# Transform work of the next batch in the drained accumulator banks: two first-stage groups or one second stage at a group's second step

## The chip, the cores and the metric

One core of one Trainium2 chip runs the kernel. The time is device microseconds of that core for one execution. The engines named below are TensorE (PE in the profile; its weight loads are PEld), VectorE (DVE), ScalarE (ACT), GpSimd (POOL) and SyncE (SP), which here issues nearly all DMAs. An engine works through its own instructions in program order and waits for others by semaphores. TensorE writes its results to PSUM, eight banks of 128 partitions by 512 fp32 numbers; ScalarE and VectorE read them there.

## The reference

```python
batch, seq, dim = (8, 3008, 256)          # d_ff = 2048, everything fp32
X = np.fft.fft(x, axis=1)
X = np.fft.fft(X, axis=2)
a = X.real.astype(np.float32)             # (8, 3008, 256) -> (24064, 256)
h = a @ w_in                              # w_in (256, 2048)
g = h * (1.0 / (1.0 + np.exp(-1.702 * h)))
out = (g @ w_out).astype(np.float32)      # w_out (2048, 256)
```

A Fourier transform over the sequence and the model dimension, of which the real part is kept, then a two-layer block with a quick GELU.

## The kernel before, in words

**Tiling.** The sequence of 3008 is 47 x 64. The transform over it is made in two stages. The *first stage* (`mix1`, L251) combines the factor 47; the *second stage* (`stage2`, L381) combines the factor 64. The transform over the model dimension is folded into `w_in` beforehand (`wcs`), so that the second stage's result `pq` is multiplied by `wcs` directly. A batch of 3008 tokens is cut into 3 blocks, a block into 2 halves, a half (a *group*) into 8 *steps* p = 0 to 7, each with two of the 16 slices of the 2048 hidden columns. That makes 48 steps a batch and 384 in all (`steps`, indexed by t; t0 = 48 b is the first step of batch b). The first 8 steps have a form of their own; t >= 8 run the loop described here. A step's tile has 256 columns, 226 in the second half of block 0.

**A step t.** PE: `begin(t, 1)` finishes the hidden values of t in a bank x (`b0` or `b1`, by t's parity), the three large products of step t-3 (`product`, with LAG = 3) go to the banks `o0` and `o1`, and `begin(t + 1)` starts the next step's hidden values. ACT: `forward` (L642), in a group's second step after it also the three copies of `swap` (L836 to L838), then `doubled` (L639), `activate_back` (L649) and `middle(t + 2)` (L627, two instructions), which writes a bias into the bank that `begin(t + 2)` will add to. DVE: `backward` (L646), the sums for the products (L664, L665; `deeper` L688, L690, L692), at a group's end the combination of its results (`combine` L799, L800; `combine_small` L828; `combine_last` L810, L846) and the transposition of the output (L779). POOL: sums (L657, L658) and the folding of the next batch's input (`fold1`).

**Small products.** The product with `w_out` is made by a fast scheme of two levels. For each pair of steps PE makes 28 products of 64 x 128 (`small_products`, L702, matmuls at L726), seven kinds k of four each, 56 instructions on the chip. They gather over a group in the tile `low`, which is three banks, and for k = 1 in half of `o1`. They go in two parts: k = 1, 2, 4, 7 three steps after the pair's second step, k = 5, 6, 3 one step later. `combine_small` reads `low` when a group has ended; from then on until the next group's first small products the three banks hold nothing that is needed. `start` of a matmul (`first_in`) clears what a bank holds.

**The next batch.** While batch b is multiplied, batch b+1 is prepared by functions that the table `extra` (filled by `at`, from `PLANS`) calls at the end of certain steps: 16 folds on POOL, 4 first-stage groups `mix1` on PE, whose result of two banks two copies on ACT (`mixed`, L279) bring back to `xt` (the first at once, the second in the next step), `spill` to DRAM, `fill` from DRAM into `t4`, `rotate`, and per block a second stage, whose two banks two transpositions on DVE (L399) bring to `pq`. `nyquist_out` and `nyquist` carry one row of it through DRAM and spread it over all partitions. `paced` is a tiny DMA that holds SP's queue until a step's activation is made. `spill`, `fill`, `load_x`, the Nyquist row and the stores are DMAs in SP's queue, in the order in which they are called.

**Banks for that.** PSUM's eight banks are `o0`, `o1`, `b0`, `b1`, `b2` and the three of `low`. A step in which `mix1` or `stage2` is called is *special*, the step after it is *after*. In a special step the two banks for it are `b2` and the x bank of step t. As that bank is not free, `middle(t + 2)` is put off to the next step, and in that step the small products are dealt out differently:

```python
if after and t + 1 < n:
    middle(t + 1)
...
cut = 0 if opening and not after else 3 if after else 2
...
if t + 2 < n and not special:
    middle(t + 2)
...
spare[:] = [f"b{t % 2}"] * special + ["b2"]
```

`opening` is the first step in which a new group's products run, that is (t - 3) % 8 == 0. Before, in batches 1 to 6, `mix1` is called at t0+7, 15, 23 and 31, and `stage2` at t0+8, 24 and 40.

Of the kernel before, what the change touches and what calls it, by code (L numbers as in the profile page):

```python
# [44 lines left out]
LAG = 3  # L45
# [76 lines left out]
def kernel(ctx: ExitStack, tc, x, w_in, w_out, tab1, tab2, out):  # L122
# [56 lines left out]
    def bank(name, tag=None):  # L179
        if tag is None:  # L180
            tag = spare.pop(0)
            spare.append(tag)
        if tag in ("o0", "o1"):
            return o_banks[int(tag[1])]
        return (rest if tag[0] == "o" else psp).tile([128, 512], F32, tag=tag, name=name)


# [88 lines left out]
    waiting = []  # L276

    def mixed(m, r, ps):
        nc.scalar.copy(free(xt[:], (4 * m + r) * D, [2 * D, 2], [1, D]), free(ps[:], 0, [D, 2], [1, D]))  # L279
# [122 lines left out]
    def nyquist(b, blk):  # L402

        nb = nbt[b, blk] = pqp.tile([128, 512], F32, tag="nb", name="nb")
        if (b, blk) != (0, 0):
            nc.sync.dma_start(out=nb[:], in_=view(Nd, (b * NBLK + blk) * 512, [0, 128], [1, 512]))
            return
        ps = bank("psn")
        halves(ps[:], ones[:], pqt[b, blk][:, 1, :], start=True, stop=True)
        nc.scalar.copy(nb[:], ps[:])  # L410


    def nyquist_out(b, blk):
        i = b * NBLK + blk
        nc.sync.dma_start(out=Nd[i:i + 1, :], in_=pqt[b, blk][0:1, 1, :])

# [140 lines left out]
    def width(t):  # L557

        return 226 if steps[t][1:3] == (0, 1) else 256
# [136 lines left out]
    def spot(pair_, k):  # L696
        return 256 + 128 * pair_ if k == 1 else 768 * pair_ + 128 * SPOT[k]

    def both(k, *dims):
        return free((o_banks[1] if k == 1 else pot["low"])[:], spot(0, k), [spot(1, k) - spot(0, k), 2], *dims)  # L700

    def small_products(t, ks):  # L702

        if t < 0 or not deep(t) or not steps[t][3] % 2:
            return
        p, w = steps[t][3] - 1, width(t) // 2
        for k in ks:
            for pr in range(2):
                for side in range(2):
                    op_ = 2 * pr + side  # L710
                    weights, q = ((wo, 2), (wo, 3), (wt, 2), (wt, 3))[op_]
                    y0, y1 = (weights[:, p + i, q, :] for i in range(2))
                    at = MADE + (p // 2 * 2 + pr) * 512 + side * 64
                    lhs = {1: y0[:, 0:64], 2: y1[:, 0:64], 3: y1[:, 64:128]}.get(k)
                    if lhs is None:
                        at += {5: 0, 6: 1, 7: 2, 4: 3}[k] * 128
                        lhs = big[:, at:at + 64]
                    raw_ = {1: (t - 1, 0), 2: (t, 0), 4: (t, 1)}.get(k)
                    if raw_:
                        rhs = right(raw_[0], op_, 256)[:, raw_[1] * w:raw_[1] * w + w]  # L720
                    else:
                        i0 = SUM + 512 * {7: 0, 5: 1, 6: 2, 3: 3}[k] + 128 * op_
                        rhs = big[:, i0:i0 + w]
                    first_in = p == 0 and (k, pr) in ((2, 0), (2, 1), (4, 1))
                    o = (o_banks[1] if k == 1 else pot["low"])[64 * side:64 * side + 64, spot(pr, k):spot(pr, k) + w]
                    nc.tensor.matmul(o, lhsT=lhs, rhs=rhs, start=first_in, stop=(p == NP - 2), skip_group_check=True)  # L726

    def small_weights(n):
# [227 lines left out]
    for h0 in (0, 512):  # L956
# [10 lines left out]
    halved(1)  # L967

    extra = {}
    PLANS = (((*range(9, 18), 22, 23, 24, 25, 26, 29, 30), (15, 17, 26, 31), 33),  # L970
             ([g + k for g in (0, 8, 16, 24) for k in range(-2, 2)], (7, 15, 23, 31), 33))

    def at(t, fn, *args):
        extra.setdefault(t, []).append((fn, args))
# [20 lines left out]
    for b in range(B):  # L995
        t0 = b * NBLK * NF
        if b + 2 < B:
            for k in range(3):
                at(t0 + 11 + k, paced, t0 + 11 + k)
                at(t0 + 11 + k, turn, b + 2, k)  # L1000
        if b + 1 < B:
            folds, groups, filled = PLANS[min(b, 1)]
            for c in range(NCH):
                for part in range(2):
                    at(t0 + folds[2 * c + part], fold1, b + 1, c, part, nc.gpsimd)
                if c % 2:
                    k = t0 + groups[c // 2]
                    at(k, mix1, b + 1, c // 2)
                    for half in range(2):
                        at(k + 1, spill, b + 1, half, c // 2)  # L1010
            for blk in range(NBLK):
                at(t0 + filled + blk, paced, t0 + filled + blk)
                at(t0 + filled + blk, fill, b + 1, 4 * blk, 4 * blk + 4)
            if b + 2 < B:
                for k in range(4):
                    at(t0 + 36 + 2 * k, paced, t0 + 36 + 2 * k)
                    at(t0 + 36 + 2 * k, load_x, b + 2, k)
                at(t0 + 34, paced, t0 + 34)
                at(t0 + 34, load_ends, b + 2)
                at(t0 + 41, fold_ends, b + 2, nc.gpsimd)  # L1020
            at(t0 + 39, rotate, b + 1)
        for blk in range(NBLK):
            nxt = (b, blk + 1) if blk + 1 < NBLK else (b + 1, 0)
            if nxt[0] < B:
                at(t0 + blk * NF + 8, stage2, *nxt)
                at(t0 + blk * NF + 9, nyquist_out, *nxt)
                at(t0 + blk * NF + 10, nyquist, *nxt)

    SCRIPT = (
        [(nyquist, 0, 0), (fold_w, 1, ("o0", "o1")), (prepare, out0), (rows, 0, ((sizes, out0, nc.vector), (clamp, out0))), (high, out0)],  # L1030
# [8 lines left out]
    for t in range(n + LAG):  # L1039
        if t < NP:  # L1040
            if t == NP - 3:
                spare[:] = [tag for tag in spare if tag[0] == "o"] + ["b2"]
            if t == NP - 1:
                middle(NP)
            hidden(t)
            if t == NP - 1:
                begin(NP)
                no_row(1024)
            for fn, *args in SCRIPT[t]:
                fn(*args)  # L1050
            if t == NP - 1:
                doubled(NP)
                middle(NP + 1)
        else:
            after, special = (any(fn in (mix1, stage2) for fn, _ in extra.get(k, ())) for k in (t - 1, t))
            if t < n:
                begin(t, 1)
            if t == NP:
                activate(t - 1)
            if after and t + 1 < n:  # L1060
                middle(t + 1)
            if t < n:
                forward(t)
            while waiting:
                m, ps = waiting.pop()
                mixed(m, 1, ps)
            opening = (t - LAG) % NP == 0 and t >= NP + LAG
            one, other = (t - LAG, (1, 2, 4, 7)), (t - LAG - 1, (5, 6, 3))
            if opening:
                small_products(*other)  # L1070
            cut = 0 if opening and not after else 3 if after else 2
            product(t - LAG, 0, cut)
            if after:
                small_products(one[0], one[1][:1])
                small_products(other[0], () if opening else other[1][:1])
            if t + 1 < n:
                begin(t + 1)
            if not opening:
                small_products(other[0], other[1][after:])
            product(t - LAG, cut, 6 if t - LAG == last else None)  # L1080
            small_products(one[0], one[1][after:])
            swap(t - LAG - 2)
            if t < n:
                backward(t)
            if t + 1 < n:
                doubled(t + 1)
            if t < n:
                activate_back(t)
                sums(t, nc.gpsimd)
            if t + 2 < n and not special:  # L1090
                middle(t + 2)
            combine_small(t - LAG - 1)
            if t - LAG == last:
                product(last, 6, None)
            sums(t - 1, nc.vector)
            deeper(t - 2, 0)
            deeper(t - 3, 1)
        if t == NP:
            psu.close()
            low = ctx.enter_context(tc.tile_pool(name="low", bufs=1, space=PS))  # L1100
            pot["low"] = low.tile([128, 3 * 512], F32, tag="low", name="low")
        if t >= LAG:
            combine(t - LAG)
            combine_last(t - LAG - 2)
            turn_last(t - LAG - 3, 0)
            turn_last(t - LAG - 4, 1)
        if t >= NP:
            spare[:] = [f"b{t % 2}"] * special + ["b2"]
        for fn, args in extra.get(t, ()):
            fn(*args)  # L1110

# [27 lines left out]
```

## Time and profile before

| | |
|---|---|
| runs | 1843.16, 1844.06, 1845.63 us; median 1844.06 us |
| profiled execution | 1846.94 us, span on the core 1845.2 us |
| granted PE clock | 0.999 |
| DVE busy | 1477.5 us (80% of the span) |
| ACT busy | 1137.2 us (62%) |
| POOL busy | 998.3 us (54%) |
| first-stage matmuls, L271, 47x256 | 434 instructions on the chip, mean 388 ns |
| second-stage matmuls, L392, 64x128 | 1536 instructions, mean 278 ns |
| first-stage copies on ACT, L279 | 56, mean 580 ns |
| second-stage transpositions on DVE, L399, 128x512 | 46, mean 696 ns |
| DMA | 105.95 MB, mean 57 GB/s |

The shares are of the span. A line of the order in time gives start, length, engine, line, operation, what it writes and reads, shape and count; in brackets the engine's idle time before it and who ended that. Neighbouring instructions of one kind are merged. One matmul of the program is two instructions on the chip, and two column halves run side by side, so lengths of matmuls overlap, and what a group costs is read from start to start.

### The profile page before, as it was taken

The page shows a single profiled execution, that of the slowest core. Times are in us where ns is not written, and L with a number is a line of the kernel's source. Part 1 is how long each engine was busy: PE and PEld are TensorE (multiplying, and loading weights), DVE is VectorE, ACT ScalarE, POOL GpSimd, SP SyncE. Part 2 cuts the span into 40 slices and gives each one's busy share as a digit, 9 for nine tenths or more (in the row PEclk, how much of TensorE's full clock was granted, in tenths as well). Part 3 has the DMA queues.
Part 4 walks back from the last instruction along what each step waited for, and adds up shares of the span by engine and source line. Part 5 has one row for each costly group of instructions (what it writes and reads, how often), then busy time and mean ns, then how long its engine had stood idle before and what let it go on. Part 6 is the DMA issues. An engine that isn't in the chain of part 4 may idle for free.

```text
span 1845.2 us, 55857 instructions
## 1 busy us (share of the span) xinstructions
PE 1827.1 (99%) x23652; PEld 1398.2 (76%) x23652; DVE 1477.5 (80%) x1934; ACT 1137.2 (62%) x2230; POOL 998.3 (54%) x1070
## 2 busy tenths in 40 slices
PE   8999999999999999999999999999999999999998
PEld 4677777777777777777777777777777777778776
DVE  6878888887888778877888778877888788878874
ACT  3666666666666666666566666666666666556663
POOL 3785556654656546564456644656446654444442
PEclk9999999999999999999999999999999999999999
DMA  8821341114211151211502115020241102100001
GB/s 263 202 70 26 86 69 28 55 32 100 49 45 43 33 114 30 60 33 42 116 14 72 30 52 97 20 74 26 71 76 27 31 26 58 29 19 13 23 19 24
DMA packets 151833, 105.95 MB, mean 57 GB/s; under 512 B 106229, under 2 KB 133111, under 8 KB 151024
## 3 DMA queue, kind: packets, MB, share of 16 engines
q1 hardware_dynamic: 148416, 99.35, 22.4%
q8 instruction: 186, 3.05, 0.7%
q10 hardware_dynamic: 3168, 3.03, 0.6%
q14 instruction: 63, 0.52, 0.1%
HBM read 65.07 MB, written 48.05 MB: 61 GB/s over the span
## 4 chain that ended last, share of the span: by engine, by line
PE 92%; POOL 2%; DVE 2%; DMA 2%; issue 2%; ACT 0%; SPq 0%; DVEq 0%; POOLq 0%; ACTq 0%
PE x L194 34%; PE o L194 25%; PE low L726 25%; PE o L726 4%; PE ps L271 2%; PE ps L392 1%; DMA big<-in_moe_w_in_dram 1%; DMA xt<-in_x_dram 1%; POOL big L658 1%; POOL big L657 0%; PE po L194 0%; DMA Tf<-big 0%; PE pa L194 0%; POOL xt L891 0%; DVE big L692 0%
## 5 line engine op out<-in xcount | busy, mean ns | idle before, releaser
L657 POOL TENSOR_TENSOR big<-big 128x256 f32<-128x256 f32 (+1 forms) x376 | 353.6, 941 | 787.6 <-ACT big L649 689.0
L194 PE MATMUL x<-pq,wcs 128*64 128x256 f32 (+1 forms) x6016 | 768.8, 376 | 1.7 <-ACT g L639 0.9
L194 PE MATMUL o<-big,wo 128*64 128x256 f32 (+1 forms) x4800 | 621.0, 375 | 0.5 <-DVE big L664 0.5
L194 PEld LDWEIGHTS x<-pq,wcs 128*64 128x64 f32 x6016 | 414.6, 137 | 181.2 <-issue 15.6
L639 ACT ACTIVATE g<-x 128x512 f32<-128x512 f32 (+1 forms) x376 | 221.7, 590 | 378.8 <-PE x L194 377.7
L194 PEld LDWEIGHTS o<-big,wo 128*64 128x64 f32 x4800 | 341.7, 137 | 147.0 <-DVE big L664 0.9
L658 POOL TENSOR_TENSOR big<-big 128x256 f32<-128x256 f32 (+1 forms) x376 | 411.1, 1093 | 0.0
L646 DVE TENSOR_TENSOR big<-g,x 128x512 f32<-128x512 f32 (+1 forms) x376 | 251.0, 667 | 185.2 <-ACT big L642 185.0
L627 ACT ACTIVATE x<-nb,af 128x256 f32<-128x256 f32 (+1 forms) x752 | 352.9, 469 | 67.8 <-DVE pq L399 54.7
L726 PE MATMUL low<-big 128*64 128x128 f32 (+1 forms) x5888 | 381.4, 270 | 0.0
L726 PEld LDWEIGHTS low<-big 128*64 128x64 f32 x5888 | 337.0, 137 | 28.1
L642 ACT ACTIVATE big<-x 128x512 f32<-128x512 f32 (+1 forms) x376 | 219.2, 583 | 121.7 <-PE x L194 110.0
L688 DVE TENSOR_TENSOR big<-big 128x1024 f32<-128x1024 f32 (+1 forms) x184 | 235.6, 1280 | 65.9 <-PE low L726 43.1
L649 ACT ACTIVATE big<-big 128x512 f32<-128x512 f32 (+1 forms) x376 | 231.6, 616 | 37.2 <-DVE big L646 35.0
L726 PE MATMUL low<-big,wo 128*64 128x128 f32 (+1 forms) x2944 | 220.2, 270 | 0.0
L690 DVE TENSOR_TENSOR big<-big 128x512 f32<-128x512 f32 (+1 forms) x184 | 177.6, 965 | 18.4 <-PE x L194 1.8
L692 DVE TENSOR_TENSOR big<-big 128x512 f32<-128x512 f32 (+1 forms) x184 | 184.2, 1001 | 0.0
L726 PEld LDWEIGHTS low<-big,wo 128*64 128x64 f32 x2944 | 171.9, 137 | 3.9 <-DVE big L692 0.3
L665 DVE TENSOR_TENSOR big<-big 128x512 f32<-128x512 f32 (+1 forms) x188 | 143.3, 762 | 6.5
L664 DVE TENSOR_TENSOR big<-big 128x512 f32<-128x512 f32 (+1 forms) x188 | 130.6, 695 | 3.5 <-POOL big L657 3.5
L828 DVE TENSOR_TENSOR big<-big,low 128x512 f32<-128x512 f32 (+3 forms) x184 | 109.0, 609 | 3.8
L726 PEld LDWEIGHTS o<-big,wo 128*64 128x64 f32 x1472 | 92.4, 137 | 24.8
(114 smaller groups left out, 1100.7 us busy)
## 6 DMA issues: line engine op xcount, KB each, us to landing
out_dram<-os SPq DMA_DIRECT2D x284, 64.0 KB
Td<-xt SPq DMA_DIRECT2D x56, 192.0 KB
t<-Td SPq DMA_DIRECT2D x21, 512.0 KB
xt<-in_x_dram SPq DMA_DIRECT2D x14, 512.0 KB
xt<-Xr SPq DMA_DIRECT2D x14, 512.0 KB
nb<-Nd SPq DMA_DIRECT2D x23, 256.0 KB
out_dram<-os SPq DMA_DIRECT2D x96, 56.0 KB
Xr<-in_x_dram SPq DMA_DIRECT2D x7, 752.0 KB
```

Of the source, the lines that this page charges most:

```text
L194: nc.tensor.matmul(out[c0:c0 + 64], lhsT=lhs[:, c0:c0 + 64], rhs=rhs, skip_group_check=True, **how)
L627: nc.scalar.activation(x[:, i * 256:i * 256 + n], nbt[b, blk][:, hh * 256:hh * 256 + n], ACTF.Copy, scale=af1[:, f:f + 1])
L639: nc.scalar.activation(two(g[:], n), two(xb[t][:], n), ACTF.Copy, scale=2.0)
L642: nc.scalar.activation(front(t), two(xb[t][:], width(t)), ACTF.Gelu_apprx_sigmoid)
L646: nc.vector.tensor_tensor(back(t), two(gt.pop(t)[:], n), two(xb.pop(t)[:], n), op=ALU.subtract)
L649: nc.scalar.activation(back(t), back(t), ACTF.Gelu_apprx_sigmoid)
L657: eng.tensor_tensor(right(t, S1, n), left(t, A21, n), right(t, A22, n), op=ALU.add)
L658: eng.tensor_tensor(left(t, S3, n), left(t, A11, n), left(t, A21, n), op=ALU.subtract)
L688: nc.vector.tensor_tensor(free(big[:], SUM, *both_), free(big[:], from11 + w, *twice), free(big[:], from11, [at_right(t, 0) + w - from11, ...
L690: nc.vector.tensor_tensor(s2, a11, s1, op=ALU.subtract)
L692: nc.vector.tensor_tensor(s4, a12, s2, op=ALU.subtract)
L726: nc.tensor.matmul(o, lhsT=lhs, rhs=rhs, start=first_in, stop=(p == NP - 2), skip_group_check=True)
```

## The change

At a group's second step (t % 8 == 4, where t - 3 is the group's p = 1), `low` has been read by `combine_small` one step before. The change makes these the only special steps, lets `mix1` and `stage2` use the banks of `low` (tags `l0`, `l1`, `l2`) and `b2` there, and has the group's first small products, all 28 of the pair, follow at the end of the next step. Since `middle(t + 2)` need not wait for a bank any more, it is always called in step t. Two first-stage groups lie in one step (t0+12 and t0+28 in batches 1 to 6; in the first batch t0+20, twice t0+28, and t0+36). Second stages are at t0+4, 20 and 36 (first batch: 8, 20, 44, where step 20 has a group as well). The Nyquist row of batch 1, block 0 is made by PE and ACT instead of by way of DRAM. `first_in` is worked out from what has been opened rather than from fixed places.

```diff
@@ bank
         if tag in ("o0", "o1"):
             return o_banks[int(tag[1])]
+        if tag[0] == "l":
+            return pot["low"][:, 512 * int(tag[1]):512 * int(tag[1]) + 512]
@@ nyquist
-        if (b, blk) != (0, 0):
+        if (b, blk) not in ((0, 0), (1, 0)):
@@ nyquist_out
+        if (b, blk) == (1, 0):
+            return
@@ small_products
+    opened = set()
...
+        if p:
+            opened.clear()
...
-                    first_in = p == 0 and (k, pr) in ((2, 0), (2, 1), (4, 1))
...
+                    place = spot(pr, k) // 512, side
+                    first_in = p == 0 and k > 1 and place not in opened
+                    if first_in:
+                        opened.add(place)
@@ the plan of a batch
-    PLANS = (((*range(9, 18), 22, 23, 24, 25, 26, 29, 30), (15, 17, 26, 31), 33),
-             ([g + k for g in (0, 8, 16, 24) for k in range(-2, 2)], (7, 15, 23, 31), 33))
+    PLANS = (((*range(9, 18), 22, 23, 24, 25, 26, 29, 30), (20, 28, 28, 36), 39, 43, (38, 40, 41, 42), (8, 20, 44)),
+             ([g + k for g in (0, 8, 16, 24) for k in range(-2, 2)], (12, 12, 28, 28), 31, 35, (36, 38, 40, 42), (4, 20, 36)))
...
-                        at(k + 1, spill, b + 1, half, c // 2)
+                        at(k + 1 + c // 2 % 2, spill, b + 1, half, c // 2)
...
-                    at(t0 + 36 + 2 * k, load_x, b + 2, k)
+                    at(t0 + loads[k], load_x, b + 2, k)
...
-            at(t0 + 39, rotate, b + 1)
+            at(t0 + turned_at, rotate, b + 1)
...
-                at(t0 + blk * NF + 8, stage2, *nxt)
-                at(t0 + blk * NF + 9, nyquist_out, *nxt)
-                at(t0 + blk * NF + 10, nyquist, *nxt)
+                k = t0 + seconds[blk]
+                at(k, stage2, *nxt)
+                at(k + 1, nyquist_out, *nxt)
+                at(k + 1 + (nxt != (1, 0)), nyquist, *nxt)
@@ the loop over steps
+            assert t == NP or not special or (t - LAG) % NP == 1
...
-            if after and t + 1 < n:
-                middle(t + 1)
+            if waiting:
+                m, ps = waiting.pop(0)
+                mixed(m, 1, ps)
             if t < n:
                 forward(t)
             while waiting:
...
-            one, other = (t - LAG, (1, 2, 4, 7)), (t - LAG - 1, (5, 6, 3))
+            one, other = (1, 2, 4, 7), (5, 6, 3)
             if opening:
-                small_products(*other)
-            cut = 0 if opening and not after else 3 if after else 2
+                small_products(t - LAG - 1, other)
+            cut = 0 if opening else 2
             product(t - LAG, 0, cut)
-            if after:
-                small_products(one[0], one[1][:1])
-                small_products(other[0], () if opening else other[1][:1])
             if t + 1 < n:
                 begin(t + 1)
-            if not opening:
-                small_products(other[0], other[1][after:])
+            if not opening and not after:
+                small_products(t - LAG - 1, other)
             product(t - LAG, cut, 6 if t - LAG == last else None)
-            small_products(one[0], one[1][after:])
+            if after:
+                small_products(t - LAG - 1, (7, *other, 1, 2, 4))
+            elif not special:
+                small_products(t - LAG, one)
...
-            if t + 2 < n and not special:
+            if t + 2 < n:
                 middle(t + 2)
...
-            spare[:] = [f"b{t % 2}"] * special + ["b2"]
+            spare[:] = ["l0", "l1", "l2", "b2"] if special else ["b2"]
```

The third numbers of `PLANS` are the step of the first `fill` (before 33; now 39 in the first batch and 31 in the others), the fourth the step of `rotate`.

More of the change, by code (lines that the diff above doesn't have):

```diff
@@ L1000 @@
                 at(t0 + 11 + k, turn, b + 2, k)
+        folds, groups, filled, turned_at, loads, seconds = PLANS[min(b, 1)]
         if b + 1 < B:
-            folds, groups, filled = PLANS[min(b, 1)]
             for c in range(NCH):
@@ L1015 @@
                 for k in range(4):
-                    at(t0 + 36 + 2 * k, paced, t0 + 36 + 2 * k)
-                    at(t0 + 36 + 2 * k, load_x, b + 2, k)
+                    at(t0 + loads[k], paced, t0 + loads[k])
+                    at(t0 + loads[k], load_x, b + 2, k)
                 at(t0 + 34, paced, t0 + 34)
```

## The prediction

> **What bounds the kernel now.** First the page: busy times and the chain that ended last.
>
> ```profile
> PE 1827.1 (99%) x23652; PEld 1398.2 (76%) x23652; DVE 1477.5 (80%) x1934; ACT 1137.2 (62%) x2230; POOL 998.3 (54%) x1070
> PE 92%; POOL 2%; DVE 2%; DMA 2%; issue 2%; ACT 0%; SPq 0%; DVEq 0%; POOLq 0%; ACTq 0%
> ```
>
> TensorE is the bound. A busy PE need not be a PE at its peak, so next comes the order in time on PE, for two ordinary steps (132 and 133 of 384; step 132 is a group's second in the sense of the change).
>
> ```profile
> 661.13 1.03 PE L194 MATMUL x<-pq,wcs 128*64 128x256 f32 x8
> 661.99 1.03 PE L194 MATMUL o<-big,wo 128*64 128x256 f32 x8
> ...
> 663.72 0.60 PE L194 MATMUL o<-big,wo 128*64 128x256 f32 x4
> 664.15 0.61 PE L726 MATMUL o<-big,wo 128*64 128x128 f32 x8
> ...
> 665.89 1.03 PE L194 MATMUL x<-pq,wcs 128*64 128x256 f32 x8
> ...
> 668.48 1.04 PE L726 MATMUL low<-big 128*64 128x128 f32 x16
> ...
> 669.79 0.60 PE L194 MATMUL o<-big,wo 128*64 128x256 f32 x4
> 670.23 1.03 PE L194 MATMUL x<-pq,wcs 128*64 128x256 f32 x8
> ```
>
> Starts follow each other without a hole: eight 256-column matmuls take 0.86 us (661.13 to 661.99). The two steps take 9.10: large products 3.02 in each (661.13 to 664.15; 665.89 to 668.48 plus 669.79 to 670.23), small products 1.74 (664.15 to 665.89) and 1.31 (668.48 to 669.79), together 3.05. So only two things move the end: a stop of PE, or the price of the inserted first-stage and second-stage work. The same view around one of each:
>
> ```profile
> 641.32 0.60 PE L194 MATMUL o<-big,wo 128*64 128x256 f32 x4
> 641.85 1.09 PE L271 MATMUL ps<-xt,w 47*64 47x256 f32 x16
> 642.88 1.08 PE L194 MATMUL x<-pq,wcs 128*64 128x256 f32 x8
> 643.79 1.47 PE L194 MATMUL o<-big,wo 128*64 128x256 f32 x12
> ```
>
> ```profile
> 683.34 1.04 PE L726 MATMUL low<-big 128*64 128x128 f32 x16
> 684.31 1.19 PE L392 MATMUL ps<-t,small 64*32 64x128 f32 x64
> 685.43 1.08 PE L194 MATMUL x<-pq,wcs 128*64 128x256 f32 x8
> ```
>
> A first-stage group costs 1.03 itself (641.85 to 642.88), 0.10 going in (0.53 from 641.32, ordinarily 0.43) and 0.05 coming out (0.91, ordinarily 0.86): **1.18**. A second stage costs 1.12 + 0.10 + 0.05, and two steps later the bias written late by ScalarE (L627) costs another 0.10 (the same view at 689.38 to 690.78): **1.37**.
>
> Last, the engines that must empty the banks, in the same step 132: VectorE, with a pair of second-stage transpositions from step 136, then ScalarE, with a first-stage copy from step 128.
>
> ```profile
> 668.02 1.30 DVE L846 TENSOR_TENSOR big<-big 128x768 f32<-128x768 f32 x1
> ...
> 685.55 1.31 DVE L399 STREAM_TRANSPOSE pq<-ps 128x512 f32<-128x512 f32 x2 [1.73 <-PE ps L392]
> ```
>
> ```profile
> 665.99 0.97 ACT L627 ACTIVATE x<-nb,af 128x256 f32<-128x256 f32 x2
> ...
> 642.98 0.59 ACT L279 COPY xt<-ps 128x512 f32<-128x512 f32 x1 [1.58 <-PE ps L271]
> ```
>
> The last operation that finishes a group's result (L846) ends at 669.32, **8.19 after the step's start**; in every group whose second step is t0+4, t0+20 or t0+36 of a batch the same view has 8.19 to 8.24 (8.50 once, in the first batch). ScalarE in that step also makes the three copies of swap, so its bias pair ends at 666.96, **5.83 after the start**. In the kernel before, neither lateness reaches PE. The change puts bank-emptying work behind both.
>
> **The change, part by part.** Let s be a special step, time 0 its start on PE.
>
> *Second stage at s.* PE runs 3.02, then 0.10 + 1.12 + 0.05, then the large products of s+1, 3.02: it reaches the small products at 7.31. In the changed kernel as built, the first of them waits for the second transposition, in VectorE's program order behind L846. Those two start where L846 lets them, 8.12 (following instructions overlap by 0.07), and end at 9.43. PE follows 0.05 later (ScalarE's L639 ends at 689.82 and PE starts at 689.87) with 0.05 on its first matmuls: 9.53, then 3.05: the pair ends at 12.58, that is 3.48 over 9.10, against 1.37 before: **+2.11**. Queued behind on VectorE are backward(s+1), then the sums of `deeper`, which wait for small products 7, 5 and 6 (1.31, to 10.84) and with a transposition of output (2.97 by the means of L688, L690 and L779) end at 13.8; the next backward can start 1.74 into its step, at 14.3, so nothing further is late. Places: second steps 8, 20, 44 in the first batch, 4, 20, 36 in six, 4, 20 in the last, 23; step 8 comes ahead of any small product, and step 20 of the first batch is counted below: 21 x 2.11 = **+44.3**.
>
> *First-stage pair at s.* The first group runs from 3.12 to 4.15. As built, the second group's first matmul waits for the copy of the first group's first bank, though it writes another bank. That copy stands on ScalarE behind forward, swap, doubled, activate_back and the bias pair: it starts at 5.83 less 0.05 and takes 0.58, so PE goes on at 6.41 after a hole of 2.26. Second group to 7.44, 0.05, large products 3.02, small products 3.05 (their wait, on the copy of the second bank, ends near 8.5 and PE comes at 10.5): 13.56, or 4.46 over 9.10, against 2 x 1.18 = 2.36: **+2.10**. Steps 12 and 28 in six batches and 28 in the first: 13 x 2.10 = **+27.3**. Step 12 is 226 columns wide; its bias pair ends at 5.53, its own work is shorter alike. The 0.31 that a pair without a hole would save (one entry, one exit, and 1.03 against 0.86 in a run) is lost in the hole.
>
> *The first batch's rest.* Step 20 has one group and a second stage that waits for that group's copy (6.21 there): 6.26 + 1.12 + 0.05 + 3.02 + 3.05 = 13.50, 4.40 over 9.10, against 2.55: +1.85. Step 36 has one group and no hole: 0.
>
> *Small edits.* The Nyquist row of (1,0) goes through PE: four 512-column instructions, 0.86 at twice the price of 256 columns, 1.0 with an entry and an exit; I take 0.9, and the two DMAs that vanish from SP's queue were hidden. The bias is no longer put off (`middle(t+2)` always runs): its 0.10 is inside 1.37. Small products a step late: the same 56 instructions, nothing by themselves; their cover is the data, made two steps before, and without it they would wait for L692, which ends 5.6 after s. DMAs, all on SP's queue: spills leave at t0+13, 14, 29, 30 (before 8, 16, 24, 32), fills at 31 to 33 (33 to 35), each still one step behind the last spill; the last fill takes 4.0 (issued 658.82, landed 662.84), some 7 before rotate at t0+35 reads it. If it came later, PE would stop for the difference, and the stores behind it on SP would wait too.
>
> Sum: 44.3 + 27.3 + 1.9 + 0.9 = **+74**. The profiled span of 1845.2 becomes 1919 (that execution took 1846.94 with what lies around the span); the median of the runs is 1.1 below the span, 1844.06, so **1918 us**.
>
> **Bounds.** The waits are unmeasured. Transpositions: if GpSimd did not slow VectorE, L688 would take 1.22 as at 650.94, not 1.55, and L810 0.69 as its fastest row, not 1.22: 0.86 less, +1.25 each; if every place were as late as t0+44 (L846 at 8.67 to 9.02), up to +2.9: 26 to 61. First-stage hole: the bias pair ends at 5.53 to 5.84: 1.8 to 2.2 each, 23 to 29. I take the rows of the places themselves. Together +51 to +92: 1895 to 1936.
>
> **Rivals.**
> (a) *The clock falls in the holes.* It fell to half for 3.4 us once inside the work, after 31.56 to 34.97:
>
> ```profile
> 31.56:34.97 3.41, 2.05 (x84) 1.70 (x84) 3.21 (x6) 0.41 (x4) 1.80 (x2) 1.00 0.89 259
> ...
> 1837.20:1840.60 3.40, 1.91 (x18) 1.01 (x14) 2.75 (x6) 0.00 (x0) 0.00 (x0) 1.00 0.00 0
> ```
>
> PE was busy 2.05 of 3.41 there (second column), much of it one-column matmuls. For: a hole of 2.2 leaves 1.2 of 3.4. Against: 1.91 busy of wide matmuls near the end did not lower it. Each fall costs half of 3.4, 1.7; at half of the 34 holes +29: 1947. The Trainium skill, "TensorE: Matmul & The Clock Gate", section "Loop structure matters more than you think", says that only PE gaps over some 3 us cool the clock; by it none of these falls and the sum stays +74, but the row at 31.56 has no gap over 0.9, so the rule alone doesn't settle it.
> (b) *Only one wait binds.* For: each rests on another engine's lateness. Transpositions alone: 44.3 + 0.9 less 13 x 0.31: 1885. Copies alone: 27.3 + 1.9 + 0.9 less 21 x 0.10: 1872.
> (c) *The other side: no hole at all.* PE then pays one entry and exit for two groups, 13 x 0.31, and no late bias, 22 x 0.10: 6.2 less, 0.9 more: 1839. It decides if the transpositions end by 7.3 and the first copy by 4.1 after s. For: the banks are drained by then, and PE is full. Against: 8.19 and 5.83, equal in every batch.
>
> **Chances.** Forecast 0.60, (a) 0.18, (b) 0.15, (c) 0.07. Forecast, most of (a) and the upper (b) lie in 1885 to 1950, my range. A measurement of this kernel tells some 0.2% from no change: slower 0.92, same 0.02, faster 0.06.
>
> **What would show it.** Right: PE idle about 2.2 before the small products after a second stage, released by the transposition; idle 2.26 between two first-stage groups, released by the copy; batches of 234 us instead of 223. Wrong: L846 ending before 6 after s, the copy ahead of the bias pair, a granted clock under 0.99, or holes on PE anywhere else, from a DMA on SP above all.

## The result and the profile after

The changed kernel takes 1945.01 us (median of four runs, 1937.64 to 1951.13), the kernel before 1844.47 in the same comparison: a ratio of 1.0544, 95% interval 1.0496 to 1.0592. It is slower by 5%; the forecast was 1918, with a range up to 1950; two of the four runs, 1950.56 and 1951.13, lie just above that range. The profiled execution has a span of 1937.4 us against 1845.2, so there are 92 us to explain where 74 were forecast.

Busy times and the chain that ended last, changed kernel:

```profile
PE 1843.9 (95%) x23656; PEld 1401.2 (72%) x23656; DVE 1510.7 (78%) x1934; ACT 1136.2 (59%) x2231; POOL 1034.9 (53%) x1070
PE 63%; DVE 17%; issue 9%; POOL 4%; ACT 4%; DMA 2%; SPq 0%; DVEq 0%; ACTq 0%; POOLq 0%
```

The work is the same (4 instructions more on TensorE), but TensorE now holds 63% of the chain instead of 92%, and VectorE 17% instead of 2%: TensorE has begun to wait for VectorE. Its waits say for what; the columns are what was waited for, the sum in us, how often, and the longest:

```profile
PE low L737 <- DVE pq L401: 38.7, 21, 2.0
PE low L273 <- ACT xt L281: 29.0, 13, 2.5
PE psr L196 <- DMA t<-Td: 3.6, 1, 3.6
...
PE low L737 <- DVE big L696: 1.9, 1, 1.9
```

(Line numbers have moved by a few: L271 is L273, L399 is L401, L692 is L696, L726 is L737, L810 is L821, L846 is L857.) The 21 waits before small products and the 13 between first-stage groups are those of the forecast. The third, 3.6 us in which `rotate` of the first batch waits for a fill, is not in it, and neither is the last, 1.9 in step 19 of the first batch; both come back below.

**The first-stage pair**, order in time on PE and on ScalarE around step 172 (which starts at 891.77):

```profile
894.89 1.09 PE L273 MATMUL low<-xt,w 47*64 47x256 f32 x16
...
898.17 0.43 PE L273 MATMUL low<-xt,w 47*64 47x256 f32 x2 [2.18 <-ACT xt L281]
...
905.32 1.03 PE L196 MATMUL x<-pq,wcs 128*64 128x256 f32 x8
```

```profile
896.63 0.97 ACT L631 ACTIVATE x<-nb,af 128x256 f32<-128x256 f32 x2
897.54 0.58 ACT L281 COPY xt<-low 128x512 f32<-128x512 f32 x1
```

The first group is done before 896. The copy of its first bank starts at 897.54, behind the bias pair, and ends at 898.12; the second group starts at 898.17, 6.40 after the step. The pair of steps lasts from 891.77 to 905.32, 13.55 us (13.56 was forecast).

**The second stage**, PE and VectorE around step 180 (start 932.71):

```profile
935.86 1.19 PE L394 MATMUL low<-t,small 64*32 64x128 f32 x64
...
942.18 1.53 PE L737 MATMUL low<-big 128*64 128x128 f32 x24 [1.85 <-DVE pq L401]
...
945.28 1.03 PE L196 MATMUL x<-pq,wcs 128*64 128x256 f32 x8
```

```profile
938.28 1.22 DVE L821 TENSOR_TENSOR big<-big 128x512 f32<-128x512 f32 x1
939.60 1.30 DVE L857 TENSOR_TENSOR big<-big 128x768 f32<-128x768 f32 x1
940.82 1.30 DVE L401 STREAM_TRANSPOSE pq<-low 128x512 f32<-128x512 f32 x2
```

The second-stage matmuls end at 937.05, but VectorE first goes through L821 and L857, and the transpositions end at 942.12, 9.41 after the step's start. The small products go on at 9.47, and the pair of steps takes 12.57 (12.58 was forecast).

**The granted clock** fell to half in nine windows of 3.41 us inside the loop over steps. Two neighbouring windows in the first-stage pair at t0+12 of batch 3, then three others (PE busy is the second column, PEclk the last but two):

```profile
815.20:818.60 3.40, 1.17 (x24) 0.68 (x22) 3.37 (x6) 3.19 (x7) 1.36 (x2) 1.00 0.67 212
818.60:822.00 3.40, 3.40 (x24) 1.77 (x26) 1.31 (x2) 1.07 (x2) 0.60 (x1) 0.51 0.03 9
...
781.10:784.50 3.40, 1.53 (x28) 1.40 (x28) 2.78 (x5) 1.25 (x3) 0.14 (x1) 1.00 0.00 0
...
340.77:344.18 3.41, 1.68 (x26) 0.84 (x22) 3.38 (x6) 3.27 (x8) 1.00 (x2) 1.00 0.51 156
...
255.44:258.85 3.41, 1.41 (x14) 0.67 (x10) 3.34 (x5) 1.96 (x4) 1.41 (x2) 1.00 0.95 187
```

The hole of 2.23 us lies wholly in the first window, where PE is busy 1.17 of 3.40; the next window runs at half clock and costs some 1.65 us (in the run with the transpositions ahead, below, a pair at t0+12 takes 14.19 with such a fall and 12.55 without). In the third line a hole leaves 1.53 of 3.40, and the clock stayed. PE's busy share alone does not decide, though: after the fourth line, with 1.68 busy, the clock fell, and after the fifth, with 1.41, it stayed. What else decides is open. The falls are at 344.18 (two windows), 426.1, 583.1, 818.6, 1054.2, 1289.7, 1525.2 and 1798.3, all whole multiples of 3.413 apart (24 from the first to the second, then 46): from 583.1 to 1525.2 they are 235.5 us apart, which is the length of a batch and 69 windows of 3.413.

### The profile page after: what moved, and what is told of

It reads as the page before. It is cut to its first block, busy times and chain, and to the rows that moved or that the text cites. A ratio compares the mean times of both kernels' runs of the same rounds, so it can differ in the third digit from the quotient of the medians.

```text
span 1937.4 us, 55798 instructions
## 1 busy us (share of the span) xinstructions
PE 1843.9 (95%) x23656; PEld 1401.2 (72%) x23656; DVE 1510.7 (78%) x1934; ACT 1136.2 (59%) x2231; POOL 1034.9 (53%) x1070
## 4 chain that ended last, share of the span: by engine, by line
PE 63%; DVE 17%; issue 9%; POOL 4%; ACT 4%; DMA 2%; SPq 0%; DVEq 0%; ACTq 0%; POOLq 0%
PE x L196 22%; PE low L737 19%; PE o L196 16%; PE o L737 3%; DVE big L839 3%; DVE big L692 2%; DVE big L650 2%; POOL big L662 2%; POOL big L661 2%; DVE big L694 2%; DVE big L696 2%; DVE pq L401 1%; DVE big L668 1%; DVE big L857 1%; DVE big L821 1%
## 5 line engine op out<-in xcount | busy, mean ns | idle before, releaser
L661 POOL TENSOR_TENSOR big<-big 128x256 f32<-128x256 f32 (+1 forms) x376 | 374.0, 995 | 841.7 <-ACT big L653 670.0
L196 PE MATMUL o<-big,wo 128*64 128x256 f32 (+1 forms) x4800 | 630.3, 376 | 0.5 <-DVE big L668 0.5
L196 PEld LDWEIGHTS x<-pq,wcs 128*64 128x64 f32 x6016 | 420.4, 138 | 186.7 <-issue 9.0
L196 PEld LDWEIGHTS o<-big,wo 128*64 128x64 f32 x4800 | 342.6, 138 | 151.7 <-DVE big L668 0.9
L737 PE MATMUL low<-big 128*64 128x128 f32 (+1 forms) x5888 | 378.9, 271 | 38.7 <-DVE pq L401 38.7
L662 POOL TENSOR_TENSOR big<-big 128x256 f32<-128x256 f32 (+1 forms) x376 | 414.7, 1103 | 0.0
L737 PEld LDWEIGHTS low<-big 128*64 128x64 f32 x5888 | 333.5, 137 | 70.5 <-DVE pq L401 48.2
L692 DVE TENSOR_TENSOR big<-big 128x1024 f32<-128x1024 f32 (+1 forms) x184 | 242.2, 1316 | 116.7 <-PE low L737 95.9
L737 PE MATMUL low<-big,wo 128*64 128x128 f32 (+1 forms) x2944 | 221.0, 271 | 1.9 <-DVE big L696 1.9
L694 DVE TENSOR_TENSOR big<-big 128x512 f32<-128x512 f32 (+1 forms) x184 | 185.5, 1008 | 16.7 <-PE x L196 0.5
L737 PEld LDWEIGHTS low<-big,wo 128*64 128x64 f32 x2944 | 171.5, 137 | 2.4 <-DVE big L696 2.4
L696 DVE TENSOR_TENSOR big<-big 128x512 f32<-128x512 f32 (+1 forms) x184 | 170.5, 927 | 0.0
L669 DVE TENSOR_TENSOR big<-big 128x512 f32<-128x512 f32 (+1 forms) x188 | 159.2, 847 | 6.5
L668 DVE TENSOR_TENSOR big<-big 128x512 f32<-128x512 f32 (+1 forms) x188 | 137.1, 729 | 3.5 <-POOL big L661 3.5
L737 PE MATMUL o<-big,wo 128*64 128x128 f32 (+1 forms) x1472 | 110.4, 271 | 0.0
```

What stands on the lines that cost most here:

```text
L196: nc.tensor.matmul(out[c0:c0 + 64], lhsT=lhs[:, c0:c0 + 64], rhs=rhs, skip_group_check=True, **how)
L661: eng.tensor_tensor(right(t, S1, n), left(t, A21, n), right(t, A22, n), op=ALU.add)
L662: eng.tensor_tensor(left(t, S3, n), left(t, A11, n), left(t, A21, n), op=ALU.subtract)
L692: nc.vector.tensor_tensor(free(big[:], SUM, *both_), free(big[:], from11 + w, *twice), free(big[:], from11, [at_right(t, 0) + w - from11, ...
L694: nc.vector.tensor_tensor(s2, a11, s1, op=ALU.subtract)
L696: nc.vector.tensor_tensor(s4, a12, s2, op=ALU.subtract)
```

## The experiments

The theory from here on has three parts. (1) Each hole is made by the order of the program: on VectorE, where the transpositions stand behind L821 and L857, and between ScalarE and PE, where the first copy is issued ahead of the second group's matmuls. (2) What makes PE wait there is not the bank but the tile `low`, of which another bank is read. (3) The rest of the loss is the clock, which falls in the holes. Rivals: the holes come from sharing the banks as such, or come back elsewhere when one is removed; and the rest is a DMA or something outside the steps.

### One wait taken away at a time, and both

**Copies behind the second group.** ScalarE's order stays, but both groups' matmuls are issued ahead of the first copies:

```diff
-        mixed(m, 0, ps[0])
+        firsts.append((m, ps[0]))
@@ the loop over steps, after the functions of extra
+        for m, ps in firsts:
+            mixed(m, 0, ps)
+        firsts.clear()
```

> Changed kernel, but the first-bank copies on ScalarE of both first-stage groups are issued after the second group's matmuls. Theory (two holes, each a fixed stop of PE): the hole between the groups goes, a special pair at t0+28 takes 3.02 + 0.10 + 1.03 + 0.86 + 0.05 + 3.02 + 3.05 = 11.13 us instead of 13.55, 13 times: -31 us; step 20 of the first batch -0.9. The second-stage pairs stay at 12.58. If the clock falls only in the longer holes at t0+12, all falls inside the work go too (9 in the profile, 1.7 each, -15): 1891; if it falls in the second-stage holes as well, about 1905. Rival (ScalarE is late as a whole, and the stop only moves to the small products or to the next x bank): 1925 to 1945, with a hole of 2 us elsewhere in steps 12, 13, 28, 29.

Measured: 1892.21 us (1889.97 to 1893.41), ratio 1.0252, interval 1.0237 to 1.0267. The first-stage pair at t0+28 takes 11.14, the waits between groups are gone from the list, and the 20 waits for transpositions that are left sum to 38.4 us. PE and ScalarE around step 172, which starts at 866.55 here:

```profile
869.67 1.30 PE L273 MATMUL low<-xt,w 47*64 47x256 f32 x18
870.60 0.38 PE L273 MATMUL ps<-xt,w 47*64 47x256 f32 x2
```

```profile
872.32 1.55 ACT L281 COPY xt<-low 128x512 f32<-128x512 f32 x3
```

The copies are as late as before, 5.77 after the step; what is gone is the second group's wait for the first of them. Not all falls went: three are left in the loop, at the stop of `rotate` and twice at t0+21, in holes of the second stage.

**Transpositions ahead of `combine_last`:**

```diff
-            combine_last(t - LAG - 2)
@@ the loop over steps, after the functions of extra
+        if t >= LAG:
+            combine_last(t - LAG - 2)
```

> Changed kernel, but combine_last is issued on VectorE after the second stage's transpositions instead of before them. Theory: the transpositions run right after L692, which ends 5.6 after the step's start, and end at 6.9, ahead of PE's arrival at 7.31: the pair takes 10.36 us instead of 12.58, 21 times: -46 us. The first-stage holes and the clock falls at t0+12 stay: 1891 in the profile, runs 1890 to 1905 with the number of falls. Rival (VectorE is simply overfull in these two steps, and combine_last, now later, makes backward and with it the x bank late): less than half of it, 1915 to 1945, with PE waiting for a bias (L631) in the steps after.

Measured: 1893.23 us (1890.73 to 1894.72), ratio 1.0257, interval 1.0242 to 1.0273. The second-stage pair takes 10.49, and the clock falls in nine windows of the loop as before. The longest line of PE's waits in this kernel, with none for a transposition in the loop:

```profile
PE low L273 <- ACT xt L281: 29.0, 13, 2.5
```

**Both edits together.**

> Both moves together. Theory: no hole is left in the special steps, the pairs take 10.36 and 11.13, the clock stays at 0.998 or more; what is left against the kernel before is -4.0 (13 first-stage pairs, one entry and exit less) -2.2 (late bias) +0.9 (Nyquist row on PE) +3.8 (rotate in the first batch waits for a fill) and perhaps +1.4 ahead of step 8: 1840 to 1846. Rival (the special steps hold more work than the three engines can take in time, so that holes reappear elsewhere): over 1860.

Measured: 1843.31 us (ten runs, 1839.83 to 1846.99) against 1846.03, ratio 0.9988, interval 0.9979 to 0.9998. VectorE and PE around the same step 180, which starts at 886.84 here:

```profile
892.40 1.31 DVE L401 STREAM_TRANSPOSE pq<-low 128x512 f32<-128x512 f32 x2
893.63 0.68 DVE L821 TENSOR_TENSOR big<-big 128x512 f32<-128x512 f32 x1
894.41 0.96 DVE L857 TENSOR_TENSOR big<-big 128x768 f32<-128x768 f32 x1
```

```profile
893.86 0.60 PE L196 MATMUL o<-big,wo 128*64 128x256 f32 x4
894.29 1.48 PE L737 MATMUL low<-big 128*64 128x128 f32 x24
```

The transpositions end at 893.71, and PE reaches the small products at 894.29 without a hole; L821 and L857, now behind, delay nobody. So part (1) is shown: the two orders make both waits, and without them the change costs nothing. Alone they gave back 52.8 and 51.8 us, together 101.7 (1945.0 to 1843.3), falls of the clock included: the two nearly add up, so neither hole hides behind the other. The banks are shared here too, so sharing as such costs nothing. A batch takes 222.7 us instead of 223.2 to 223.7 before.

### Bank or tile

The first group of a pair now gets `b2` and bank 0 of `low`, the second banks 1 and 2. ScalarE's order is that of the changed kernel:

```diff
-            spare[:] = ["l0", "l1", "l2", "b2"] if special else ["b2"]
+            spare[:] = ["b2", "l0", "l1", "l2"] if special else ["b2"]
```

> Changed kernel, only the order of the four banks differs: the first bank handed out in a special step is b2, which is a tile of its own, then the three of low. Theory (the second first-stage group waits because the copy of the first bank reads the same tile low, not because the bank itself is in use): the copy made in the special step now reads b2, so the second group starts at once and the hole of 2.3 to 2.5 us goes. The small products then wait for the last copy of low, which stands behind forward on ScalarE and ends at about 8.6 us after the step's start, where PE comes at 8.1: a new hole of about 0.5. 13 pairs x (2.43 - 0.55): -24 us, and the clock falls at t0+12 go: about 1897 to 1915 with the falls that the second-stage holes bring about. Rival (the wait is for ScalarE's work as such): the hole stays, 1935 or more.

Measured: 1905.12 us (1901.41 to 1906.55), ratio 1.0320, interval 1.0306 to 1.0334. The first copy still stands behind the bias pair, but now it reads `b2`, and the second group no longer waits for it. PE and ScalarE around step 172, which starts at 874.00 here:

```profile
877.83 1.25 PE L273 MATMUL low<-xt,w 47*64 47x256 f32 x18
879.00 1.08 PE L196 MATMUL x<-pq,wcs 128*64 128x256 f32 x8
```

```profile
878.86 0.97 ACT L631 ACTIVATE x<-nb,af 128x256 f32<-128x256 f32 x2
879.77 0.58 ACT L281 COPY xt<-ps 128x512 f32<-128x512 f32 x1
```

The pair at t0+28 takes 11.45, 0.31 more than with the copies behind, and that at t0+12 takes 10.76 instead of 10.09: the small products now wait for a copy. The line of it holds the six waits at t0+13, some 0.45 each, and one of 2.0 in the first batch; at t0+29 they are too short to be listed:

```profile
PE low L737 <- ACT xt L281: 4.6, 7, 2.0
```

So part (2) is shown for the first-stage pair: a matmul into one bank of `low` waits for the read of another bank of `low` and not for that of `b2`, with nothing else changed. The holes of the second stage remain; the clock now falls there, at t0+21, in six of the eight batches (that step then takes 10.02 instead of 8.38).

### Holes filled

What do the holes cost apart from their length? Useless matmuls, two of 128x512, are put into the hole between two first-stage groups (`steps_now` holds the step at hand):

```diff
+        if firsts and firsts[-1] == steps_now[0]:
+            warm(2, "b2")
+        firsts[:] = steps_now
```

> Changed kernel with two useless 128x512 matmuls (four instructions on the chip, about 1.7 us) between the two first-stage groups of a pair, where PE otherwise waits 2.3 to 2.5 us for the copy. Theory of the clock (it falls when PE's work in a stretch of 3.4 us is under some 0.36, which only the holes at t0+12 bring about): the pairs stay at 13.55, the falls inside the work go although PE does more: 1922 in the profile (1937.4 less 9 x 1.7), and the runs lie close together instead of 13 apart. Rival (the falls come from something else, or from both kinds of hole): falls stay, 1935 or more.

Measured: 1931.11 us (1926.25 to 1935.84), ratio 1.0463, interval 1.0439 to 1.0488: 14 us under the changed kernel by the medians and 8 by the profiled spans (1929.2 and 1937.4), but not the forecast 1922, and the falls did not end. They left t0+12 and came up in the hole of the second stage, six in the loop instead of nine. The windows there:

```profile
1085.90:1089.30 3.40, 1.37 (x20) 0.85 (x18) 3.15 (x5) 0.71 (x2) 0.00 (x0) 1.00 0.00 0
1089.30:1092.70 3.40, 3.40 (x36) 3.40 (x34) 2.58 (x2) 1.36 (x3) 2.40 (x2) 0.51 0.00 0
```

A batch still takes 235.46 us. My expectation that only the hole at t0+12 matters was wrong: either kind of hole can make the clock fall, and which one does depends on where the windows lie. So both were filled:

```diff
+                if any(fn is stage2 for fn, _ in extra.get(t - 1, ())) and t > 21:
+                    warm(2, "b2")
```

> Changed kernel with the useless matmuls in both kinds of hole: between the two first-stage groups, and before the small products in the step after a second stage (where PE waits 2.2 us for the transpositions). Theory (the clock falls wherever a stretch of 3.4 us holds too little work of PE, in whichever hole the stretches happen to lie): no fall inside the work except perhaps at rotate in the first batch, every batch 1 to 6 takes 233.8 us, 1918 to 1923 in the profile, runs within 3 us of each other. Rival (falls come from something else): one fall a batch stays, 235.4 a batch, 1929 or more.

Measured: 1922.70 us (1918.95 to 1925.87), ratio 1.0412, interval 1.0396 to 1.0428. PE does more work, and the kernel is 22 us faster than the changed one. The runs lie 6.9 apart, not within the 3 expected. Four of the six batches take 233.78 to 233.80 (the others 234.05 and 233.72), where the forecast without a fall gives 223.26 + 3 x 2.11 + 2 x 2.10 = 233.8. The one fall left inside the loop follows the stop at `rotate`:

```profile
PE psr L196 <- DMA t<-Td: 3.8, 1, 3.8
```

So part (3) is shown for the falls: with both holes filled they go, and a batch takes what its holes alone explain. The stop at `rotate` and the start of the loop are not the clock; they are counted below.

### The fill that came late

In the kernel with both orders moved, the first batch alone still takes 198.0 us instead of 190.9. Its four loads of the batch after next go out behind the fills instead of between them:

```diff
-    PLANS = ((..., (20, 28, 28, 36), 39, 43, (38, 40, 41, 42), (8, 20, 44)),
+    PLANS = ((..., (20, 28, 28, 36), 39, 43, (41, 42, 43, 44), (8, 20, 44)),
```

> Both moves, and in the first batch the loads of the batch after next go behind the fills in SP's queue (steps 41 to 44 instead of 38 and 40 to 42). Theory (the third fill is late because the large loads are ahead of it in the queue, and rotate at step 43 stops PE for 3.5 us, which also makes the clock fall): the stop at step 43 goes (-3.9) and the two fallen windows behind it (-2.6): 1837 in the profile, 0.3 to 0.4% under the kernel before. Rival (the fill itself takes as long, whatever is ahead of it; or GpSimd's folds at step 46 now wait for the loads and hold the sums up): 1842 or more.

Measured: 1842.43 us (eleven runs, 1841.86 to 1845.11) against 1845.4, ratio 0.9984, interval 0.9976 to 0.9993. The stop of `rotate` is gone (step 43 takes 4.42 instead of 8.28), the clock does not fall inside the loop, and the first batch takes 194.3. That is 3.7 us, not the expected 6.5: two new holes in steps 44 and 46 take back 2.5 us. The profiled span is 1842.4, not the expected 1837.

```profile
PE x L196 <- issue: 1.4, 1, 1.4
PE low L394 <- issue: 1.1, 1, 1.1
```

The profile shows nothing that these wait for. They fall while the moved loads run, but that the loads cause them wasn't tried and stays open. The third fill now leaves 2.04 after the start of step 41, where it left 6.7 after it with the loads between, and `rotate` comes 11.4 after that: enough time even for a fill that takes 10.6. So the run does not tell whether the loads also make the fill itself slower. This is the fastest version here, and its interval lies below 1; at 0.16% the gain is still under the 0.2% named as the bound for a measurement of this kernel.

## Why the prediction was right, and where it was short

- **The time: inside the range, but above the forecast's own sum.** The bounds worked out for the two waits ended at 1936; 1945 lies in the range because the range took in most of rival (a). Both waits came at their places and sizes, and that is no luck; that the range held owes something to a rival that was given 0.18.
- **Second stage, +2.11 at 21 places: right.** Pair of steps 12.57 (forecast 12.58), transpositions at 9.41 (9.43), all 21 places in the list of waits; at one of them, the first batch's t0+44, the wait is only 0.26, behind the stop at `rotate`. That VectorE's program order is the cause, and L857's lateness with it, is shown by moving `combine_last`.
- **First-stage pair, +2.10 at 13 places: right.** 13.55 against 13.56 at t0+28, PE on again at 6.40 against 6.41; at t0+12 the pair without a fall takes 12.55, 4.50 over the 8.05 before, where 4.46 was forecast. The forecast said that the wait is on the copy "though it writes another bank"; the run with another bank order shows that this is so.
- **First batch's step 20:** 13.50 as forecast. **Step 36:** no hole, as forecast. **Nyquist row on PE:** 0.86 from its first matmul to the next step's start; 0.9 was taken.
- **The clock: the forecast's central case left it out, and rival (a) was partly true.** The nine windows at 1.65 are 15 us in the profiled span. Rival (a) had it in half of 34 holes, 17, and was given 0.18. In the profiled run it is about one fall per batch: from batch 2 to 6 a batch, its fall included, is a whole number of windows long (69) and so meets them at the same place each time. The runs of the changed kernel lie in two pairs, 1938 to 1939 at granted clocks of 0.990 and 0.991, and 1951 at 0.982 and 0.984. At 0.983 the half-speed time is 2 x 0.017 x 1949 = 66 us or 19 windows, at 0.9905 it is 37 us or 11: eight more falls at 1.65 are 13 us, the distance between the pairs. Where the extra falls lie was not looked at, since only one of these runs has a profile. The argument against the rival, that 1.91 busy of 3.41 had not lowered the clock, was true and didn't reach far enough: a hole of 2.2 leaves 1.2.
- **The Trainium skill's rule** against throughput drops ("TensorE: Matmul & The Clock Gate", section "Why this matters for your kernels"), "No PE-idle gaps >~3µs between matmul bursts", is too wide a bound here: holes of 2.0 to 2.2 us brought the clock down, and filling them ended it. The measurement decides.
- **The last fill: this step failed.** The forecast said "the last fill takes 4.0 (issued 658.82, landed 662.84), some 7 before rotate at t0+35 reads it". That was worked out for batches 1 to 6 alone. In the first batch the fills go out at t0+39 to 41 and `rotate` comes at t0+43, with loads between them on SP's queue. The changed kernel, DMA issues of SP and then PE:

```profile
248.08 0.35 SPq L218 DMA_DIRECT2D xt<-in_x_dram  x1
248.47 0.91 SPq L218 DMA_DIRECT2D xt<-Xr  x1
249.91 0.39 SPq L374 DMA_DIRECT2D t<-Td  x1
```

```profile
260.47 0.29 PE L196 MATMUL psr<-t,small 128*64 128x12 f32 x4 [3.62 <-DMA t<-Td]
```

  SP's own waits in this stretch hold what comes before that:

```profile
SPq L422 <- DMA Tk<-big: 10.1, 2, 5.9
```

  Steps 40 and 41 call `paced` twice, once for a fill and once for a load. The second tiny DMA writes where the first does and waits for it to land: SP's queue stood for 5.9 us, from 241.9 to 247.82, and the third fill left 6.66 after the start of step 41 instead of 2.04 as in the run with the loads behind. The matmul that waits for it then starts 10.6 us after the fill's issue, where 4.0 was taken. How much of that is due to the two loads of 512 KB each that leave just ahead of it stays open: the run with one hole filled has the same order, and there the matmul came 6.8 after the fill's issue without a wait. Step 43 takes 8.26 instead of 4.33; about 1.6 came back in the next two steps (11.85, where 12.58 and 0.86 for the Nyquist row were due). The forecast had named such a stop as what would make it wrong, without working it out for the batch where the times differ.
- **A hole that nobody forecast.** In step 19 of the first batch the small products wait 1.9 for VectorE's sum L696, the last line of the waits above; the step takes 6.27 instead of 4.18, in every version with the change. It hardly shows in the total, because two holes of the kernel before are gone from the first batch: step 8 takes 6.20 instead of 7.25, step 27 4.33 instead of 5.31. Why VectorE is late in step 19 was not tested.

Together: 74 as forecast, 15 for the clock, 3.9 less 1.6 for the fill, and a loop that starts 1.4 later (81.3 instead of 79.9) make 92.7; the span grew by 92.2. The hole in step 19 and the two that went, +2.1 and -2.0, are left out of this sum. The loop's start lay between 76.8 and 81.3 in the runs here, and is put to no part of the change. The medians differ by 100.5, since the median of the four runs lies between the two pairs.

## What to carry to other kernels

Banks that are empty are not free for use until the engine that must empty them again comes to it in its own program order: look at what stands ahead of the read on that engine before placing work there, and issue the read first or put other work behind it. A tile that spans several banks orders writers and readers of different banks behind each other, so either issue all its writers before its first reader, or let the first reader have a tile of its own. A short hole on TensorE can cost nearly twice its length through the clock. A loop whose period is a whole number of clock windows meets them at the same place in every turn, for better or worse: the changed kernel's 235.5 us fell in each batch from 2 to 6, and the 228.9 us of the run with the copies behind (some 67 windows) fell once in batches 1 to 6, though it kept its second-stage holes of some 2 us. And a slack worked out for the steady loop must be worked out again for its first turn.

## What was not expected of the hardware

The granted clock went to half for one window of 3.41 us after windows in which PE was busy 1.17 to 1.37 of 3.40, with no gap longer than 2.23 us. There is no sharp bound of the busy share: the clock also fell after 1.68 of 3.41 and stayed after 1.41 and 1.53. Useless matmuls in the holes made the kernel 22 us faster (1945.0 to 1922.7). A loop of 235.5 us, 69 such windows, repeated its fall in every batch from 2 to 6.
